# Where chunk 3 is transposed, where raw copies lie, and which bank comes next: three edits in the second layer's projection of a two-layer transformer kernel

## The chip, the cores and the metric

The kernel runs on one core of a Trainium2 chip. The metric is the device time of one execution in microseconds; the median of three runs before the change is 1957.98 us (1957.88 to 1958.28).

The core's engines are named as in the profile: PE (TensorE, matmuls and transposes through the array) with PEld (its weight loads), ACT (ScalarE), DVE (VectorE), POOL (GpSimd) and SP (SyncE, which here only issues DMAs). Each engine works through its own list of instructions in order and waits on semaphores for the others. TensorE writes to eight PSUM banks of 128 x 512 fp32 words; ACT and DVE copy from there to SBUF.

## The reference

Two layers of attention and two of feed-forward alternate, on one sequence of 2048 positions with 448 features, in fp32, with the same weights both times:

```python
x = x + A(layernorm(x))      # 16 heads of 28, one key and one value head for all
x = x + B(layernorm(x))      # (silu(x @ w_gate) * (x @ w_up)) @ w_down, 1792 wide
x = x + A(layernorm(x))
x = x + B(layernorm(x))

def A(x):
    q = x @ wq               # split into 16 heads of 28
    k, v = x @ wk, x @ wv    # 28 wide, shared by the heads
    p = softmax(q @ k.T * 28 ** -0.5)
    return concat(p @ v) @ wo
```

## The kernel before, in words

The sequence is cut into four chunks of 512 positions (`NC`), each of four tiles of 128. To keep fp32 accuracy in matmuls, each operand is split into a high part, rounded to the matmul's format, and the rest (`xh`, `xl`; `wh`, `wl`). A projection of one chunk by 128 columns of weights (`product_T`, L304) is 11 matmuls into one bank: three for each of three blocks of 128 features, and two for the last block of 64, which holds both parts stacked.

A layer's attention has 16 projection steps (`Attention.project`, L496), four chunks by four column blocks `m`; `self.seen` counts them, and this text calls them steps 0 to 15. Step n belongs to chunk n // 4. A column block holds 112 columns of queries and 16 of the keys (m = 2, 3) or of the values (m = 0, 1). A step (`q`, L516) takes a bank, runs the 11 matmuls, and then:

- ACT casts the bank to the high part of the queries (`self.hi`, L538) and copies it whole to a raw tile (L539). The raw tile comes from a pool `stage` of two, which the feed-forward also uses; for chunk 3 of the second layer it is one of four slices of an `xn` tile (L528 to L531).
- SP stores the raw tile's queries to DRAM (`qd`, L540), and its keys to `kt` (L543), or DVE transposes the values (L546) and POOL copies them into `vsb` (L549).
- After steps 6, 10 and 14 TensorE multiplies a chunk's queries with a few keys (`maxima`, L434), and DVE reduces that to a bound for the softmax and SP stores it.

Besides, `self.when` holds what is to be issued after a step of a given number: loads of keys and queries back from DRAM on SP (L398, L421, L432), and their splits on POOL (L135, L136).

The steps need a chunk's normalised rows transposed, features on partitions. In the second layer this is done in two ways. Chunks 0 to 2 go through DRAM: DVE transposes 32 x 32 blocks (`turn_tile`), SP stores them (`send`), loads them back in the wanted order (`load`, L944), and `halved` (L286) splits them, the high parts by casts on ACT (L292, L296), the rests by subtractions on DVE (L293, L302). Chunk 3, which the feed-forward ends with, goes through TensorE: `flip` (L243) makes 16 transposes of 128 x 128, four to a bank, and for each bank ACT casts (L254, L258) and DVE subtracts (L255, L264).

The order is written out by hand; instructions run on each engine in the order in which the Python code issues them. Steps 0 to 3 of the second layer are spread over the last units of the first feed-forward (`hand_over`, L910, through `self.soon`, and `rest`, L1083); the rest follows in `finish` (L553), behind the feed-forward's last products. `hand_over` puts further pieces into `self.plan`, keyed by the step and by 0 (before its matmuls) or 1 (behind them): for chunk 2 the load behind step 4 and the split before step 7, for chunk 3 the last of the normalisation (`ready`: DVE L230, POOL L232) behind step 5. `project` calls `turned` for a chunk before the step ahead of its first and before its first: chunk 3's `flip` comes before step 11. The rows then are TensorE's transposes (L248), ahead of step 11's matmuls.

`bank(cands)` (L111) hands out banks in turn, with one position kept for each list of candidates, and skips those held. `finish` sets the list for steps 4 to 12 and for the flip: 0 to 7 in order. Steps 13 to 15 take 3, 4, 5, and `maxima` has a list of its own. Steps 2 and 3 took banks 1 and 2 of the four low ones, so `used`, of which the change speaks, is 2. Before the change steps 4 to 10 have banks 0 to 6, the flip 7, 0, 1, 2, steps 11 and 12 banks 3 and 4; the three `maxima` have 4, 5, 6.

`halves` (L122) is a pair of 128 x 512 tiles under one tag with two buffers. The feed-forward keeps its product `h` in it (`h2`, L1017), the attention its sums (`o2`, L694).

Behind step 15 the scores begin (`scores`, L566): in each cycle TensorE makes 24 matmuls of scores (L633) and 8 of the products with the values (L688), ACT three exponentials (L655, L656).

Of the kernel before, what the change touches and what calls it, by code (L numbers as in the profile page):

```python
# [8 lines left out]
F32 = mybir.dt.float32  # L9
# [14 lines left out]
NC = S // 512  # L24
# [31 lines left out]
def forward(  # L56
# [32 lines left out]
    LOW, HIGH, ALL = (0, 1, 2, 3), (4, 5, 6, 7), (4, 5, 6, 7, 0, 1, 2, 3)  # L89
    wide = [ALL]  # L90
# [20 lines left out]
    def bank(cands, hold=False):  # L111

        for _ in cands:
            turn[cands] = (turn.get(cands, -1) + 1) % len(cands)
            b = cands[turn[cands]]
            if b not in live:
                if hold:
                    live.add(b)
                return b, banks[b]
        raise AssertionError("no bank")  # L120

    def halves(name):  # L122

        return pers.tile([P, 2, 512], F32R, tag="halves", name=name, bufs=2)
# [151 lines left out]
    def natural(po, squares):  # L276

        if not squares:
            return po
        return po.rearrange("p (g t w) -> p t g w", g=4, w=32)  # L280

    def in_order(a, squares):

        return a.rearrange("p (t g w) -> p t g w", g=4, w=32) if squares else a
# [19 lines left out]
    def product_T(po, a_h, a_l, tiles):  # L304

        xh, xl = tiles[:2]
        seq = []
        for k in range(3):
            seq += [(a_h[k], xh[:, k, :]), (a_h[k], xl[:, k, :]), (a_l[k], xh[:, k, :])]
        seq += [(a_h[3], xh[:, 3, :]), (a_l[3], xh[:, 3, :])]  # L310
        for i, (a, b) in enumerate(seq):
            nc.tensor.matmul(po, a, b, start=(i == 0), stop=(i == len(seq) - 1))
# [30 lines left out]
    class Attention:  # L343
# [152 lines left out]
        def project(self):  # L496

            c, m = self.order[self.seen]
            for f in self.plan.get((self.seen, 0), ()):
                f()  # L500
            late = self.layer == 0 and self.seen == 3
            turned = [self.order[n][0] for n in (self.seen, self.seen + 1) if n % 4 == 0 and n < len(self.order)]
            for o in turned if not late else ():
                self.turned(o)
            self.q(c, m)
            for o in turned if late else ():
                self.turned(o)
            for f in self.plan.get((self.seen, 1), []) + self.when.pop(self.seen, []):
                f()
            self.seen += 1  # L510
# [5 lines left out]
        def q(self, c, m):  # L516
            cs = slice(512 * c, 512 * c + 512)
            sq = c in self.squares
            held, po = bank((3, 4, 5) if self.seen > len(self.order) - 4 else wide[-1], True)
            ms = slice(P * m, P * m + P)  # L520
            wh, wl = self.w
            product_T(po, [wh[:, k, ms] for k in range(4)], [wl[:, k, ms] for k in range(4)], self.X[c])
            if not full and self.seen in (6, 10, 14):
                self.maxima(self.seen // 4 - 1)()
            live.remove(held)
            if c not in self.qd:
                self.qd[c] = dram.tile([D, 512], F32, name=f"qd{self.layer}_{c}")
            if self.layer and c == NC - 1:  # L528
                if "xn" not in self.spare:
                    self.spare["xn"] = pers.tile([P, 4, 512], F32, name="xn")  # L530
                raw = self.spare["xn"][:, self.seen % 4, :]  # L531
            else:
                raw = self.pool.tile([P, 512], F32, name="stage")
            if not full:
                if self.seen % 2 == 0:
                    self.two = wpool.tile([P, 2, 512], F32R, tag="wgh", name="q2", bufs=FG + 1)
                self.hi[c, m] = self.two[0:112, self.seen % 2, :]
                nc.scalar.copy(in_order(self.hi[c, m], sq), natural(po[0:112, :], sq))  # L538
            nc.scalar.copy(in_order(raw, sq), natural(po, sq))  # L539
            nc.sync.dma_start(self.qd[c][112 * m : 112 * m + 112, :], raw[0:112, :])  # L540
            d0, n = 16 * (m % 2), 12 if m % 2 else 16
            if m > 1:
                nc.sync.dma_start(self.kt[c][d0 : d0 + n, :], raw[112 : 112 + n, :])  # L543
                return
            vt = wpool.tile([P, 512], F32R, tag="wgl", name="vt", bufs=FG + 1).bitcast(F32)[96:128, :]
            nc.vector.transpose(vt, po[96:128, :])  # L546
            vt = vt.rearrange("p (u t d) -> p u t d" if sq else "p (t u d) -> p u t d", t=4, u=4)
            for u in range(4):
                nc.gpsimd.tensor_copy(  # L549
                    vsb[32 * u : 32 * u + 32, 4 * c : 4 * c + 4, d0 : d0 + n], vt[:, u, :, 16 : 16 + n]  # L550
                )

        def finish(self):  # L553

            wide.append((0, 1, 2, 3, 4, 5, 6, 7) if self.layer else ALL)
            if self.layer:
                nc.scalar.activation(warm, halfn[:, 0:1], AF.Exp)
            while self.seen < len(self.order):
                self.project()
            for n in sorted(self.when):  # L560
                for f in self.when[n]:
                    f()
            self.advance(len(self.steps), NM + KC * LEAD)
            wide.append(LOW)

        def scores(self, ff, xb):  # L566
            next(switch)
            inner = ExitStack()
            with tc.tile_pool(name=f"ow{self.layer}", bufs=1, side="right", reuse_waits="tile") as ow:
# [56 lines left out]
                def tile_scores(n, three, one):  # L626

                    i, kt = divmod(n, NT)
                    q, k, ks = qts[i % 3], keys[kt // 4], slice(P * (kt % 4), P * (kt % 4) + P)
                    for z, (kp, part) in enumerate(((0, 0), (1, 0), (0, 1))):  # L630
                        for j in (0, 1, 2, 3) if n % 2 else (3, 0, 1, 2):
                            js = slice(32 * j, 32 * j + 32)
                            nc.tensor.matmul(  # L633
                                three[:, j, :] if j < 3 else one, k[js, kp, ks], q[js, part, :],
                                start=(z == 0), stop=(z == 2), tile_position=(32 * j, 0),
                            )
                    pt, pt1 = bufs[n % 4], pairs[n // 2 % 2][:, n % 2, :]
                    pts[n] = [*(pt[:, j, :] for j in range(3)), pt1]
                    return pt, pt1
# [489 lines left out]
    for c in range(1, NC):  # L1129
        fs, got = norm_steps(c)  # L1130
        n = 4 * c - 4
# [38 lines left out]
```

## Time and profile before

| | |
|---|---|
| median of the runs | 1957.98 us |
| the profiled execution | 1958.55 us |
| its span, first to last instruction | 1956.8 us |
| PE busy | 1942.8 us, 99% |
| ACT busy | 1262.7 us, 65% |
| DVE busy | 969.6 us, 50% |
| POOL busy | 553.9 us, 28% |
| granted clock of TensorE, mean | 0.999 |

The profile is one execution, the time of the instructions on each engine. A busy time of TensorE is not all work at full speed: where the granted clock is below 1.00, a matmul takes longer and counts as busy all the same. In the order of time a row has the start, the duration (of the group, where "x3" stands behind it), engine, line, operation, output and inputs by their names in the program, and in brackets the idle time before it with what ended it. A row of stretches has the stretch, its length, the busy time and count of PE, weight loads, DVE, ACT and POOL, the granted clock, the busy share of the DMA engines, and GB/s.

The second layer's projection (steps 4 to 15) lies between 993.59 and 1032.87 us of the span.

### The profile page before, as it was taken

Reading aid. Unit: us, or ns where it says so; the run is one execution under the profiler, and the core shown is the slowest. Engines: PE = TensorE matmul, PEld = TensorE weight load, DVE = VectorE, ACT = ScalarE, POOL = GpSimd, SP = SyncE. Lnnn points to the kernel's source line nnn. Section 1 sums busy time; section 2 is a strip of 40 time slices with the busy share of each in tenths; the row PEclk is TensorE's granted clock in tenths of the full one; section 3 lists DMA queues with packets and bytes.
Section 4 is the critical chain, followed back from the end, with each engine's and each line's share of the span. In section 5 each row is a group of like instructions: output and inputs, shape, how many; then the busy total and the mean of one; then the engine's idle time right before and its main releaser. Section 6 shows DMA issues by size and latency. Waiting matters only on the chain. (4 is left out here: it accounts for less than half of the span.)

```text
span 1956.8 us, 43898 instructions
## 1 busy us (share of the span) xinstructions
PE 1942.8 (99%) x18425; PEld 1328.7 (68%) x18425; DVE 969.6 (50%) x1639; ACT 1262.7 (65%) x1877; POOL 553.9 (28%) x592
## 2 busy tenths in 40 slices
PE   9999999999999999999999999999999999999998
PEld 7544545445468999999974445454454789988887
DVE  6666575665643222322655555657656432232323
ACT  4899898998953333333349998989989333333332
POOL 4213123122214333433341221122231342333420
PEclk9999999999999999999999999999999999999999
DMA  5111011121130011100251110110221201011102
GB/s 167 55 35 30 21 39 41 27 55 39 25 87 25 17 32 32 33 22 22 70 156 36 34 34 20 42 38 24 57 50 32 72 18 31 17 32 32 32 1 77
DMA packets 100642, 83.60 MB, mean 43 GB/s; under 512 B 25080, under 2 KB 81656, under 8 KB 100440
## 3 DMA queue, kind: packets, MB, share of 16 engines
q1 hardware_dynamic: 98744, 79.32, 14.7%
q8 instruction: 145, 2.38, 0.5%
q10 hardware_dynamic: 1696, 1.43, 0.2%
q14 instruction: 57, 0.47, 0.1%
HBM read 57.38 MB, written 21.50 MB: 40 GB/s over the span
## 5 line engine op out<-in xcount | busy, mean ns | idle before, releaser
L655 ACT ACTIVATE pt<-three 128x1536 f32<-128x1536 f32 x512 | 726.9, 1499 | 52.8 <-PE three L633 52.8
L688 PE MATMUL bank<-pt,vsb 128*32 128x512 f32 x3072 | 490.8, 598 | 0.0
L688 PE MATMUL bank<-pair,vsb 128*32 128x512 f32 x1024 | 487.4, 598 | 0.6 <-ACT pair L656 0.6
L633 PE MATMUL bank<-qstack,keys 32*128 32x512 f32 x1536 | 473.3, 425 | 0.0
L332 PE MATMUL bank<-xh,wgh 64*128 64x512 f32 x1712 | 446.7, 389 | 0.0
L633 PE MATMUL three<-qstack,keys 32*128 32x512 f32 x4608 | 428.6, 408 | 0.5 <-ACT xn L539 0.3
L633 PEld LDWEIGHTS bank<-qstack,keys 32*128 32x128 f32 x1536 | 243.3, 183 | 250.4 <-issue 123.3
L654 DVE COPY pair<-bank 128x512 f32<-128x512 f32 x512 | 354.2, 692 | 95.2 <-PE bank L633 58.9
L332 PE MATMUL bank<-xh,wgl 64*128 64x512 f32 x1391 | 368.3, 390 | 0.0
L332 PE MATMUL bank<-xl,wgh 64*128 64x512 f32 x1284 | 335.2, 389 | 0.0
L332 PE MATMUL bank<-wdh,h 64*128 64x448 f32 x1760 | 328.3, 363 | 0.0
L1022 DVE TENSOR_TENSOR sg<-bank,sg 128x512 f32<-128x512 f32 x112 | 77.4, 691 | 500.7 <-ACT sg L1021 495.8
L656 ACT ACTIVATE pair<-pair 128x1024 f32<-128x1024 f32 x256 | 285.4, 1115 | 0.0
L332 PEld LDWEIGHTS bank<-xh,wgh 64*128 64x128 f32 x1712 | 265.1, 184 | 15.6 <-issue 1.3
L633 PEld LDWEIGHTS three<-qstack,keys 32*128 32x128 f32 x4608 | 261.0, 183 | 13.9 <-DVE xres L604 1.5
L688 PEld LDWEIGHTS bank<-pt,vsb 128*32 128x32 f32 x3072 | 101.7, 109 | 246.2 <-issue 153.2
L896 POOL TENSOR_TENSOR xres<-stage,xres 128x448 f32<-128x448 f32 x107 | 126.5, 1204 | 492.8 <-ACT stage L895 492.6
L697 DVE TENSOR_TENSOR o<-bank,o 128x512 f32<-128x512 f32 x224 | 154.9, 692 | 203.7 <-PE bank L688 203.7
L332 PEld LDWEIGHTS bank<-wdh,h 64*128 64x128 f32 x1760 | 244.6, 184 | 11.6 <-issue 2.0
L339 ACT COPY seen<-bank 128x1 f32<-128x1 f32 x654 | 80.7, 163 | 250.4 <-PE bank L332 247.5
L332 PEld LDWEIGHTS bank<-xh,wgl 64*128 64x128 f32 x1391 | 218.1, 184 | 13.4
L332 PE MATMUL bank<-wdl,h 64*128 64x448 f32 x880 | 218.3, 366 | 0.0
(149 smaller groups left out, 2118.8 us busy)
## 6 DMA issues: line engine op xcount, KB each, us to landing
o<-rd SPq DMA_DIRECT2D x32, 256.0 KB
qraw<-qd SPq DMA_DIRECT2D x128, 56.0 KB
qd<-stage SPq DMA_DIRECT2D x28, 224.0 KB
wdr<-in_B_w_down_dram SPq DMA_DIRECT2D x28, 224.0 KB
xt<-tb SPq DMA_DIRECT2D x24, 224.0 KB
wr<-in_B_w_gate_dram SPq DMA_DIRECT2D x28, 192.0 KB
wr<-in_B_w_up_dram SPq DMA_DIRECT2D x28, 192.0 KB
xn<-xt SPq DMA_DIRECT2D x6, 768.0 KB
```

The lines of the kernel that those rows point to most:

```text
L332: nc.tensor.matmul(po, a, b, start=start, stop=stop, skip_group_check=True)
L339: nc.scalar.copy(seen[:, i : i + 1], po[:, 0:1])
L633: nc.tensor.matmul(three[:, j, :] if j < 3 else one, k[js, kp, ks], q[js, part, :], start=(z == 0), stop=(z == 2), tile_position=(32 * j, 0),)
L654: copies.append(nc.vector.tensor_copy(pt1, one))
L655: es.append(nc.scalar.activation(pt, threes[y], AF.Exp, scale=SCALE))
L656: es.append(nc.scalar.activation(pair, pair, AF.Exp, scale=SCALE))
L688: nc.tensor.matmul(to[32 * j : 32 * j + 32, :], vsb[:, n % NT, :], pts[n][j], start=(y == 0), stop=(y == 1), skip_group_check=True,)
L697: f = nc.vector.tensor_tensor(accs[i][:, 0, :], to, accs[i][:, 0, :], ALU.add)
L896: nc.gpsimd.tensor_tensor(r, s, r, ALU.add)
L1022: nc.vector.tensor_tensor(in_order(sg, sq), natural(pg[1], sq), in_order(sg, sq), ALU.mult)
```

## The change

Three edits, all of which act in the second layer alone (`self.layer` is 1):

- before step 8, `project` transposes chunk 3 (`NC - 1`), and no longer before step 11, where `turned` finds the chunk's rows gone and does nothing;
- the raw tiles of steps 4 to 11 are the two halves of a `halves` pair, a new pair at each even step, instead of `stage` tiles (chunk 3, steps 12 to 15, keeps its `xn` slices);
- `q` notes the bank that it held, and `finish` makes the list of banks from it: the four low ones, beginning with the one behind the last used, and then 4 to 7. With `used` = 2 that is 3, 0, 1, 2, 4, 5, 6, 7.

With it steps 4 to 7 have banks 3, 0, 1, 2, the flip 4 to 7, steps 8 to 11 again 3, 0, 1, 2, step 12 bank 4.

```diff
@@ project
             late = self.layer == 0 and self.seen == 3
             turned = [self.order[n][0] for n in (self.seen, self.seen + 1) if n % 4 == 0 and n < len(self.order)]
+            if self.layer and self.seen == 8:
+                turned = [NC - 1]
             for o in turned if not late else ():
                 self.turned(o)
             self.q(c, m)
@@ q
             product_T(po, [wh[:, k, ms] for k in range(4)], [wl[:, k, ms] for k in range(4)], self.X[c])
+            self.used = held
             if not full and self.seen in (6, 10, 14):
                 self.maxima(self.seen // 4 - 1)()
@@ q
                     self.spare["xn"] = pers.tile([P, 4, 512], F32, name="xn")
                 raw = self.spare["xn"][:, self.seen % 4, :]
+            elif self.layer and self.seen > 3:
+                if self.seen % 2 == 0:
+                    self.spare["raw"] = halves("raw").bitcast(F32)
+                raw = self.spare["raw"][:, self.seen % 2, :]
             else:
                 raw = self.pool.tile([P, 512], F32, name="stage")
@@ finish
-            wide.append((0, 1, 2, 3, 4, 5, 6, 7) if self.layer else ALL)
+            wide.append((*((self.used + n) % 4 for n in range(1, 5)), *HIGH) if self.layer else ALL)
```

## The prediction

> **What bounds the kernel now.** I read the page first (busy time, slices), then busy time by stretch around the second layer's projection, then the order of time of each engine there. A "step n" is the projection counted n in the code (16 steps per layer).
>
> The page's engine rows say that TensorE is what the time is made of, and ScalarE what it alternates with:
>
> ```profile
> PE 1942.8 (99%) x18425; PEld 1328.7 (68%) x18425; DVE 969.6 (50%) x1639; ACT 1262.7 (65%) x1877; POOL 553.9 (28%) x592
> ```
>
> Only 14.0 us of the span of 1956.8 are without a matmul, so a change that removes waits has little to win. The stretches (length, then busy time of PE, weight loads, DVE, ACT, POOL, then granted clock) show where the change's stage stands in this:
>
> ```profile
> 8.00:12.00 4.00, 2.65 (x19) 1.84 (x18) 1.78 (x4) 2.88 (x5) 2.82 (x6) 1.00 0.51 118
> 1004.85:1007.24 2.39, 0.50 (x1) 0.19 (x1) 2.26 (x6) 1.67 (x3) 0.64 (x1) 0.98 0.93 261
> 1007.24:1010.70 3.46, 3.46 (x8) 2.76 (x9) 1.93 (x3) 1.19 (x3) 1.93 (x4) 0.52 0.54 176
> 1034.00:1100.00 66.00, 65.89 (x724) 30.23 (x728) 40.06 (x65) 66.00 (x56) 8.15 (x9) 1.00 0.11 30
> 1580.00:1950.00 370.00, 370.00 (x3306) 329.66 (x3303) 109.36 (x160) 118.65 (x445) 112.12 (x91) 1.00 0.10 29
> ```
>
> From 1004.85 to 1007.24 TensorE has 0.50 us of work, and in the 3.46 us behind it "busy" hides a loss: the clock is 0.52. From 1034 on ScalarE is busy without a gap (66.00 of 66.00), and the last stage is matmul without a gap (370.00 of 370.00). So what the projection wins or loses moves the start of the scores, and the end of the kernel with it. TensorE's rows, in order of time (start, duration, what; in brackets the idle time before and its releaser):
>
> ```profile
> 1004.46 0.39 PE L312 MATMUL bank<-xh,wl 128*128 128x512 f32 x1
> 1006.13 0.50 PE L312 MATMUL bank<-xh,wh 128*128 128x512 f32 x1 [1.29 <-ACT xh L292]
> 1007.24 0.80 PE L312 MATMUL bank<-xl,wh 128*128 128x512 f32 x1 [0.60 <-DVE xl L293]
> ...
> 1010.94 0.39 PE L312 MATMUL bank<-xh,wl 128*128 128x512 f32 x1
> 1011.17 0.40 PE L312 MATMUL bank<-xh,wh 128*128 128x512 f32 x1
> ...
> 1016.18 1.10 PE L438 MATMUL bank<-q,kdiag 112*128 112x512 f32 x4
> 1017.11 1.91 PE L248 MATMUL bank<-ident,xn 128*128 128x128 f32 x16
> 1018.78 0.48 PE L312 MATMUL bank<-xh,wh 128*128 128x512 f32 x1
> ...
> 1023.67 0.39 PE L312 MATMUL bank<-xh,wl 128*128 128x512 f32 x1
> 1024.17 0.50 PE L312 MATMUL bank<-xh,wh 128*128 128x512 f32 x1
> 1024.51 0.40 PE L312 MATMUL bank<-xl,wh 128*128 128x512 f32 x1
> ...
> 1032.87 0.49 PE L633 MATMUL bank<-qstack,keys 32*128 32x512 f32 x1
> ```
>
> Step 7 ends with the matmul at 1004.46; step 8, the first of chunk 2, starts at 1006.13 and step 9 at 1011.17, where 11 matmuls at the undisturbed spacing (1010.94 to 1011.17, 0.23) would have taken 2.5 us. The transposes of chunk 3 take 1017.11 to 1018.78, ahead of step 11. Step 13 starts 0.27 us late (1023.67 + 0.23 = 1023.90, it starts at 1024.17). A first matmul behind a break has 0.1 us more to its second (1024.17 to 1024.51: 0.34). The scores begin at 1032.87.
>
> **The change part by part.** *The transposes move from before step 11 to before step 8.* They leave their old place: 1.67 us, and the 0.1 us of the restart behind them: 1.77 us. In the new place they run from 1004.46 + 0.23 = 1004.69 to 1006.36. They need chunk 3's normalised rows and a free bank; the rows of ScalarE, VectorE and GpSimd in that stretch:
>
> ```profile
> 1005.47 1.86 ACT L292 CAST xh<-qstack 128x512 fp32r<-128x512 f32 x3 [1.85 <-DMA qstack<-xt]
> 1007.74 0.62 ACT L296 CAST xh<-qstack 128x512 fp32r<-128x512 f32 x1 [0.41 <-DMA qstack<-xt]
> 1008.27 0.58 ACT L538 CAST q<-bank 112x512 fp32r<-112x512 f32 x1
> 1011.71 0.59 ACT L539 COPY stage<-bank 128x512 f32<-128x512 f32 x1 [2.86 <-DMA kt<-stage]
> 1012.19 0.59 ACT L538 CAST q<-bank 112x512 fp32r<-112x512 f32 x1
> ...
> 1017.86 1.57 ACT L254 CAST xh<-bank 128x512 fp32r<-128x512 f32 x3
> 1019.30 0.63 ACT L258 CAST xh<-bank 128x512 fp32r<-128x512 f32 x1
> ```
>
> ```profile
> 1003.39 0.70 DVE L440 STREAM_TRANSPOSE sg<-bank 128x512 f32<-128x512 f32 x1
> ...
> 1006.50 1.98 DVE L293 TENSOR_TENSOR xl<-qstack,xh 128x512 fp32r<-128x512 f32 x3
> 1008.51 0.69 DVE L302 TENSOR_TENSOR xh<-qstack,xh 64x512 fp32r<-64x512 f32 x1
> 1012.33 0.72 DVE L546 STREAM_TRANSPOSE vt<-bank 32x512 f32<-32x512 f32 x1 [3.13 <-ACT stage L539]
> ...
> 1020.51 1.89 DVE L255 TENSOR_TENSOR xl<-bank,xh 128x512 fp32r<-128x512 f32 x3
> 1022.43 0.69 DVE L264 TENSOR_TENSOR xh<-bank,xh 64x512 fp32r<-64x512 f32 x1
> 1023.39 0.72 DVE L546 STREAM_TRANSPOSE vt<-bank 32x512 f32<-32x512 f32 x1 [0.26 <-issue]
> ```
>
> ```profile
> 1002.27 1.51 POOL L232 COPY xn<-xn 128x64 f32<-128x64 f32 x4 [0.61 <-DVE xn L230]
> ```
>
> The rows are whole at 2.27 + 1.51 = 1003.78. The first bank the transposes take is that of the maxima before, read by L440 until 1004.09. Both are ahead of 1004.69, by 0.9 and 0.6 us; were that cover gone, each tenth past it would come off the start of step 8 only beyond the next bound.
>
> That bound is the load of chunk 2, which the change doesn't hasten. Step 8's first matmul can go at 1006.36 (its operand is cast by 1005.47 + 1.86/3 = 1006.09). Its second needs the first of the three subtractions, 1006.50 + 0.66 = 1007.16: it goes at 1007.24, as now. The third comes 0.34 later, the next six 0.23 apart, to 1008.96; the tenth needs L302 (1008.51 + 0.69 = 1009.20), so 1009.26; the eleventh 0.33 later, and step 9 at 1009.82. Against 1011.17 that is 1.35 us, if the clock stays full.
>
> *The clock.* It went to 0.52 behind two idle times, 1.29 and 0.60 us, with one matmul between. In the new order only 1006.75 to 1007.24 (0.5 us) is idle there. The row of 8 to 12 us has 1.35 us idle and a clock of 1.00, so 0.5 should leave it. The ends are 1.35 us (full clock) and 0 (half clock until the same moment, 1010.70: step 9 then stays at 1011.17). I take 1.35: 0.5 is far from 1.9 and below 1.35. [...]
>
> *What the transposes carry with them on the other queues.* On ACT four casts (1017.86 to 1019.93, 2.07 us) go ahead of step 8's two copies, on DVE four subtractions (1020.51 to 1023.12, 2.61 us) behind step 7's transpose L546. No DMA and no GpSimd work moves. ACT: step 7's cast ends at 1008.85, its raw copy follows at once (below), to 1009.4, the four casts to 1011.5, step 8's cast to 1012.1, its raw copy to 1012.7, where that cast now starts at 1012.19: ACT is level with before by step 9, with TensorE 1.35 us ahead. DVE: L546 at 1009.4 instead of 1012.33, the subtractions by 1012.8; its next work is the maxima of step 10, about 1015.6. Chunk 3 is ready some 5 us before step 12 (1018.3). Cost: nothing, hidden in ACT's 2.86 us and DVE's 3.13 us of waiting.
>
> *Raw copies into the double buffers of h, steps 4 to 11.* Two pairs give four places instead of two. Steps 4 to 7 no longer wait for stores; step 7's copy loses its 2.86 us. Steps 8 and 9 take the first pair and wait for the stores of steps 4 and 5, the last of which landed at 1011.71 and leaves SP in the same order: hence the raw copy above no earlier than 1011.71. The pairs' former contents (h of the last two units) are read by matmuls that stand ahead of step 4 in TensorE's own order. TensorE waits for none of these copies in the trace except through a bank.
>
> *Banks by last use.* Step 13 takes bank 3, now that of step 11 (the list of L555 turned on by L113 to L119), whose L546 ends at 1023.39 + 0.72 = 1024.11, hence 1024.17. After the change bank 3 belongs to steps 4 and 8, empty by 1012.7. The wait goes: 0.27 + 0.11 of restart = 0.38 us. Step 14's bank (4, step 12) is as near as before; next late is the scores' own start behind step 15's copies, unchanged.
>
> Sum: 1.77 + 1.35 + 0.38 = 3.50 us. The profiled execution took 1958.55 us, 1.75 outside its span, 0.57 above the median of the runs; it would become 1955.05, and the median 1957.98 - 3.50 = 1954.5.
>
> **The rivals.** *1, the clock halves all the same:* step 8 goes on at half speed until 1010.70, whatever stood before it, step 9 stays at 1011.17, and the gain is 1.77 + 0.38 = 2.15: 1955.8. For it: the one matmul of half a microsecond before 1007.24 may not count as activity, and the trace can't show what a transpose counts; against it: 1.35 us idle at full clock.
>
> *2, chunk 2's load lands earlier:* step 8 follows the transposes unbroken, ends 0.87 us sooner (1006.36 + 0.1 + 2.5 = 1008.95 for step 9), 1953.6. Against it: the load's place in SP's queue is the same, and two ACT rows wait for it (1.85, 0.41).
>
> *3, it does not do what it says:* the transposes are held (bank or rows) until chunk 2 is in, and run before step 8 outside the gap. Then 1.67 is lost there and 1.77 + 0.38 won elsewhere: 1957.5. For it only margins of 0.6 and 0.9 us.
>
> *4, slower:* step 8's raw copy waits for both stores of a whole pair, and everything on ACT is behind it. TensorE feels it when step 13 wants bank 3, at 1009.82 + 4 x 2.5 + 0.93 for the maxima (1016.18 to 1017.11) = 1020.75. To lose what is won this copy would have to be released 3.5 us past that, at about 1024.2 instead of 1011.71; at 1028.2 the kernel would be 0.2% slower, 1962. Against it: the last of the four stores had landed at 1011.71, by ACT's own row, and nothing is put ahead of it on SP.
>
> **How the numbers follow.** Forecast 0.70 (own range 1954.0 to 1955.1, for the clock's edge and the restarts), rival 1 0.13, rival 2 0.06, rival 3 0.06, rival 4 0.05. The range 1953.5 to 1956.8 takes in the forecast and rivals 1 and 2. 0.2% is 3.9 us, about what a measurement of this kernel can tell from no change: faster is rival 2 and the forecast's edge, 0.12; slower most of rival 4, 0.05; the rest, 0.83, lies within.
>
> **What would show it.** Right: 16 transposes at about 1004.7 and 1.7 us long; step 8's second matmul still at 1007.2, behind L293; a clock of 1.00 from 1007 to 1011; step 9 at 1009.8; step 11 straight behind the maxima at 1015.7; step 13 without a wait; the scores at 1029.4 instead of 1032.87, and the same length from there to the end. Wrong: a clock of 0.5 there (rival 1), transposes waiting for a bank or GpSimd (3), a raw copy on ACT past 1020 (4), or a later stage that eats the 3.5 us.

## The result, and the profile after

The changed kernel takes 1954.86 us (median of 19 runs, 1954.06 to 1957.93) beside 1958.49 us for the kernel before on the same chip (19 runs, 1957.73 to 1963.68). The ratio is 0.998, with a 95% interval of 0.9974 to 0.9987: 3.6 us faster by the medians, and inside 0.2%. The prediction had 1954.5 and 3.50 us.

The profiled execution took 1956.43 us, 1.6 above that median. Its rows around the second projection stand 1.64 us later than those before (step 7's last matmul at 1006.10, where it was 1004.46), for a reason at the start of the kernel that the last section shows. So rows of the two kernels are compared here by their distance from step 7's last matmul. TensorE, in order of time (start, duration, instruction; in brackets the idle time before it and its releaser):

```profile
1006.10 0.39 PE L312 MATMUL bank<-xh,wl 128*128 128x512 f32 x1
1006.33 1.91 PE L248 MATMUL bank<-ident,xn 128*128 128x128 f32 x16
1007.99 0.48 PE L312 MATMUL bank<-xh,wh 128*128 128x512 f32 x1
1008.90 0.50 PE L312 MATMUL bank<-xl,wh 128*128 128x512 f32 x1 [0.42 <-DVE xl L293]
...
1011.47 0.40 PE L312 MATMUL bank<-xh,wh 128*128 128x512 f32 x1
...
1016.50 1.10 PE L438 MATMUL bank<-q,kdiag 112*128 112x512 f32 x4
1017.43 0.40 PE L312 MATMUL bank<-xh,wh 128*128 128x512 f32 x1
...
1022.44 0.39 PE L312 MATMUL bank<-xh,wh 128*128 128x512 f32 x1
...
1030.97 0.50 PE L640 MATMUL bank<-qstack,keys 32*128 32x512 f32 x1
```

The transposes follow step 7 without a break. Of the two waits at step 8 one of 0.42 us is left. Step 9 (1011.47) is 5.37 us behind the mark, where it was 6.71. Step 11 follows the maxima at once, step 13 (1022.44) has no wait, and the scores begin 24.87 us behind the mark, where it was 28.41: 3.54 us won. From there to the end of the span it is 1954.7 - 1030.97 = 923.7 us, before 1956.8 - 1032.87 = 923.9: nothing is given back.

The busy time by stretch after the change (length, then busy PE, weight loads, DVE, ACT, POOL, then granted clock):

```profile
1006.50:1008.90 2.40, 1.98 (x18) 1.66 (x16) 2.27 (x6) 1.75 (x3) 0.65 (x1) 1.00 0.87 236
1008.90:1012.36 3.46, 3.46 (x14) 2.63 (x15) 3.37 (x6) 3.16 (x8) 1.93 (x4) 1.00 0.57 181
1012.36:1030.97 18.61, 18.61 (x82) 15.04 (x81) 9.85 (x17) 7.90 (x15) 14.06 (x30) 1.00 0.52 157
1032.00:1098.00 66.00, 65.80 (x720) 30.11 (x720) 40.10 (x64) 66.00 (x56) 8.82 (x9) 1.00 0.11 30
```

In 3.46 us, where TensorE did 8 matmuls at a clock of 0.52, it now does 14 at 1.00; and behind it there is no idle time at all up to the scores. ScalarE after the change:

```profile
1007.08 1.82 ACT L292 CAST xh<-qstack 128x512 fp32r<-128x512 f32 x3 [2.45 <-DMA qstack<-xt]
...
1010.21 0.59 ACT L546 COPY raw<-bank 128x512 f32<-128x512 f32 x1
1010.68 1.57 ACT L254 CAST xh<-bank 128x512 fp32r<-128x512 f32 x3
1012.11 0.63 ACT L258 CAST xh<-bank 128x512 fp32r<-128x512 f32 x1
1012.59 0.64 ACT L545 CAST q<-bank 112x512 fp32r<-112x512 f32 x1
1013.38 0.59 ACT L546 COPY raw<-bank 128x512 f32<-128x512 f32 x1
```

Step 7's raw copy (1010.21) no longer waits for a store, the four casts of chunk 3 follow it, and step 8's raw copy starts at 1013.38 - 1.64 = 1011.74 on the time scale of before, where step 5's keys landed at 1011.71 (its row names no releaser, so that it waits for them is not shown).

### The profile page after: what moved, and what is told of

Its sections match the earlier page's. It is cut to its first block, busy times and chain, and to the rows that moved or that the text cites. A ratio compares the mean times of both kernels' runs of the same rounds, so it can differ in the third digit from the quotient of the medians.

```text
span 1954.7 us, 43894 instructions
## 1 busy us (share of the span) xinstructions
PE 1942.0 (99%) x18425; PEld 1325.5 (68%) x18425; DVE 970.0 (50%) x1639; ACT 1261.9 (65%) x1877; POOL 552.8 (28%) x592
## 5 line engine op out<-in xcount | busy, mean ns | idle before, releaser
L663 ACT ACTIVATE pair<-pair 128x1024 f32<-128x1024 f32 x256 | 280.6, 1096 | 0.0
```

The source lines that it names most:

```text
L663: es.append(nc.scalar.activation(pair, pair, AF.Exp, scale=SCALE))
```

## The experiments

Each was read in two ways: its time against the kernel before on the same chip, and its TensorE rows. The table has the starts in us behind step 7's last matmul; the last column is the length to the first matmul of the scores, the mark in the expectations.

| kernel | step 8 | step 9 | 12 | 13 | 14 | 15 | scores |
|---|---|---|---|---|---|---|---|
| before | 1.67 | 6.71 | 16.95 | 19.71 | 22.38 | 25.81 | 28.41 |
| after | 1.89 | 5.37 | 13.85 | 16.34 | 18.83 | 22.27 | 24.87 |
| flip_only | 1.89 | 5.37 | 13.81 | 20.70 | 24.87 | 28.32 | 30.93 |
| flip_raw | 1.89 | 5.37 | 13.82 | 16.31 | 18.81 | 22.24 | 24.85 |
| flip_banks | 1.89 | 5.36 | 13.82 | 16.31 | 21.63 | 26.76 | 29.38 |
| raw_banks | 2.45 | 6.97 | 17.19 | 19.68 | 22.18 | 25.61 | 28.21 |
| raw_only | 1.85 | 6.19 | 17.05 | 19.58 | 22.23 | 25.66 | 28.26 |
| banks_only | 1.58 | 6.77 | 17.03 | 19.52 | 22.02 | 25.45 | 28.05 |
| filler | 1.89 | 5.37 | 15.62 | 18.83 | 21.36 | 24.80 | 27.40 |
| half | 1.75 | 5.38 | 14.73 | 17.70 | 20.22 | 23.65 | 26.26 |
| quarter | 1.69 | 5.33 | 15.11 | 18.15 | 20.67 | 24.11 | 26.71 |
| load_early | 1.89 | 5.36 | 13.82 | 16.31 | 18.81 | 22.24 | 24.85 |
| rows_late | 2.33 | 5.54 | 14.01 | 16.50 | 19.00 | 22.43 | 25.03 |
| both | 1.89 | 4.50 | 12.94 | 15.44 | 17.93 | 21.37 | 23.97 |

### The transposes alone

The first of the three edits, without the others: raw copies in `stage` tiles, banks 0 to 7.

```diff
 turned = [self.order[n][0] for n in (self.seen, self.seen + 1) if n % 4 == 0 and n < len(self.order)]
+if self.layer and self.seen == 8:
+    turned = [NC - 1]
```

> Chunk 3's transposes before step 8, raw copies in the stage tiles and banks in order as before. The mark is the length from step 7's last matmul to the first matmul of the scores: 28.41 us before (1004.46 to 1032.87), 24.87 with all three edits (1006.10 to 1030.97). Theory 'the terms add' (the prediction's): 28.41 - 1.77 - 1.35 = 25.3, and a time 3.1 us below before. Rival 'the stores bind': step 11's raw copy still waits for the store of step 9's keys, which leaves SP behind the load of keys and lands 18 us behind the mark (1022.7 in the profile before), so step 13 gets bank 3 no sooner than before: 28.0 to 28.4, and the time of before.

Measured: 1960.9 us beside 1958.94 (ratio 1.0008, 0.9999 to 1.0018), and 30.93 us from the mark to the scores, 2.5 more than before. Neither theory had it this long. Up to step 12 everything is won that was predicted (13.81 against 16.95). Then, in TensorE's rows:

```profile
1020.56 0.39 PE L312 MATMUL bank<-xh,wl 128*128 128x512 f32 x1
1025.18 0.79 PE L312 MATMUL bank<-xh,wh 128*128 128x512 f32 x1 [4.23 <-DVE vt L549]
1025.77 0.63 PE L312 MATMUL bank<-xl,wh 128*128 128x512 f32 x1
```

Step 13 wants bank 3 and stands 4.23 us for the transpose of step 11's values. What that waits for is on ScalarE (first fence), and the store in question on SP (second):

```profile
1011.95 0.59 ACT L542 COPY stage<-bank 128x512 f32<-128x512 f32 x1 [2.98 <-DMA kt<-stage]
...
1017.88 0.59 ACT L542 COPY stage<-bank 128x512 f32<-128x512 f32 x1 [0.96 <-DMA kt<-stage]
1018.49 0.59 ACT L541 CAST q<-bank 112x512 fp32r<-112x512 f32 x1
1023.73 0.58 ACT L542 COPY stage<-bank 128x512 f32<-128x512 f32 x1 [4.65 <-DMA kt<-stage]
```

```profile
1017.79 0.43 SPq L546 DMA_DIRECT2D kt<-stage  x1
```

Step 11's raw copy stands 4.65 us until step 9's keys, issued at 1017.79, have landed: 5.9 us for 32 KB. TensorE had become faster, and the landing did not come sooner for it: it came 19.25 us behind the mark, where it was 18.26 (1022.72 - 1004.46). So step 11 waits for what step 9 left behind. The rival had this wait, and left out two things: the landing 1 us later, for which no run shows the reason, and a second bill. Behind the idle time the granted clock is 0.61 over 4.22 us, where it was 0.99:

```profile
1020.60:1025.18 4.58, 0.35 (x2) 0.00 (x0) 0.72 (x1) 1.45 (x3) 0.63 (x3) 0.99 0.51 154
1025.18:1029.40 4.22, 4.22 (x12) 3.36 (x13) 0.72 (x1) 0.11 (x1) 3.65 (x10) 0.61 0.36 109
```

From step 13 to 14 it then takes 4.17 us instead of 2.50. The wait of 4.39 us (20.70 against 13.81 + 2.50) and this 1.67 are the 6.06 us by which the length stands above that of all three edits.

### The transposes with the pairs, and with the banks

> The transposes before step 8 and the raw copies in the pairs, banks in order as before. 'The terms add': the 0.38 us of the banks is missing, 25.3. 'The stores bind': with no raw copy waiting for a store, step 11's bank 3 is empty before step 13 asks for it, and the banks are worth nothing beside the pairs: 24.9, 3.5 us below before.

Measured: 1955.44 us beside 1958.94 (0.9983, 0.9974 to 0.9993), length 24.85, the changed kernel's to 0.02. With the pairs, the banks are worth nothing here.

> The transposes before step 8 and the banks by last use, raw copies in the stage tiles. 'The terms add': the pairs had no term of their own, 24.9. 'The stores bind': step 13 finds bank 3 empty, but ACT stands at step 11's raw copy until the same store has landed, step 12's bank 4 is emptied behind it, and step 14 waits for that: 26.5 to 26.8, 1.6 to 1.9 us below before.

Measured: 1959.49 us (1.0, 0.9991 to 1.001), length 29.38. Step 13 finds its bank, as both theories have it, but step 14 does not: ScalarE stands at step 11's raw copy as above, and step 12's bank, which it would empty behind that, comes late.

```profile
1025.77 0.52 PE L312 MATMUL bank<-xh,wh 128*128 128x512 f32 x1 [2.66 <-DVE vt L549]
```

The 2.8 us of this wait (21.63 against 18.81) and 1.7 us of a lower clock behind it (0.67 from 1025.77 to 1031.00; 14 to 15 takes 5.13, where it is 3.43 with the maxima between) make 4.5, the distance to the changed kernel. The stores bind; moving the bank moves the wait by one step.

### The pairs and the banks without the transposes

> The pairs and the banks, the transposes left before step 11. Both theories: only step 13's wait goes, 28.03; step 8 with the same gap (1.29 and 0.60 us) and the clock at half behind it. If the clock stays full here, the gap was not its cause, and the length is 26.7.

> The pairs alone: transposes before step 11, banks in order as before. Step 13 still takes step 11's bank 3. If the store that step 11's raw copy waits for made bank 3 late, that wait goes with the pairs as it does with the banks: 2.5 us from step 12's first matmul to step 13's, where it was 2.76 before. If it needs the banks: 2.76 as before. The gap at step 8 and the half clock stay in any case, step 9 at 6.7 to 7.0 behind step 7's last matmul.

> The banks by last use alone: transposes before step 11, raw copies in the stage tiles. Step 13 gets a bank that has long been empty: 2.5 us from step 12's to step 13's first matmul, and a length of 28.0. ACT still stands at step 11's raw copy (0.5 us before); if that now holds up step 14, whose bank 4 is emptied behind it, 13 to 14 is longer than 2.5.

Measured: raw_banks 1958.07 us beside 1958.94 (0.9992, 0.9982 to 1.0001), length 28.21; raw_only and banks_only, one execution each, lengths 28.26 and 28.05. Step 12 to 13 is 2.49, 2.53 and 2.49 where it was 2.76: either edit takes that wait away, and together they do it once. In raw_only step 14 then starts 0.15 late, and the length gains 0.15 against 0.36. raw_banks is 0.16 longer than banks_only; chunk 2's load landed later in its execution (step 8 at 2.45 instead of 1.58). All three keep the gap at step 8 and a lower clock behind it (0.57 in raw_banks, 0.68 in raw_only, 0.56 in banks_only, over some 3.5 us).

### What the transposes are worth as activity

The pairs and banks, chunk 3's transposes left before step 11, and 16 transposes of the identity in the new place; they are added work, and nothing reads them.

```diff
+if self.layer and self.seen == 8:
+    for n in range(16):
+        nc.tensor.transpose(banks[7][:, 0:P], ident, ident)
```

> The pairs and the banks, chunk 3's transposes left before step 11, and in their new place 16 transposes of the identity into a bank that nobody reads: work for TensorE in the gap that brings nothing. If the activity in the gap keeps the clock up (the prediction's term of 1.35 us): a clock of 1.00 from step 8 on, step 9 some 5.36 us behind step 7's last matmul, and a length of 28.03 - 1.35 = 26.7. If the clock does not depend on that gap: half clock behind it, step 9 at 6.71 as before, 28.03.

Measured: step 9 at 5.37 as in the changed kernel, at a clock of 1.00 from 1006.77 to 1010.20: the term of 1.35 us comes of the filled gap, also where the work in it is useless. The length is 27.40, 0.7 more than expected: with steps 9 and 10 earlier and the real transposes where they were, chunk 3's subtractions on VectorE, behind the maxima of step 10, come too late for step 12 (a wait of 0.34 us for L255, and more behind it). The time (1958.67 beside 1959.03; 0.9999, 0.9989 to 1.0008) can't tell this from before. So 1.35 us of earlier steps is not 1.35 us of the kernel while the transposes stay ahead of step 11.

Half of the transposes (two banks of four), then a quarter, ahead of step 8, the others before step 11:

```diff
+if self.layer and self.seen == 8:
+    flip(self.norms[NC - 1], self.X[NC - 1], (0, 1))     # half; (0,) in quarter
 def turned(self, c):
     if c in self.norms:
-        flip(self.norms.pop(c), self.X[c])
+        flip(self.norms.pop(c), self.X[c], (2, 3) if self.layer else range(4))     # (1, 2, 3) in quarter
```

> All three edits, but only half of the transposes (two of four banks) before step 8, the other half before step 11. The gap then has 0.8 and some 0.5 us idle. If that little leaves the clock up, as the 1.35 us idle in the first layer did: 24.87 + 0.84 + 0.1 = 25.8. If it halves behind it: step 9 at 6.71, 27.2.

> All three edits, one of the four banks of transposes before step 8, three before step 11. About 1.5 us of 2.4 are then idle around step 8's first matmul, between the 1.0 that left the clock up and the 1.9 that halved it. Clock full: step 9 at 5.4 behind step 7's last matmul. Clock halved: 6.7 to 7.0. [...]

Measured: half 1956.75 us beside 1959.03 (0.9988, 0.9978 to 0.9997), length 26.26; quarter, one execution, 26.71. In both step 9 is at 5.4 and the clock behind the gap 1.00 (half 1010.63 to 1014.10, quarter 1007.34 to 1010.80). half is 0.5 us longer than expected, for filler's reason: from step 12 to 13 it takes 2.97 us instead of 2.50 (VectorE's last two subtractions end at 1024.18 and 1024.90, and the matmuls behind them start at 1024.24 and 1024.96). The stretches from step 7's end to step 8's second matmul, and the 3.5 us behind them, for quarter, raw_only, banks_only and raw_banks:

```profile
1004.97:1007.34 2.37, 0.93 (x6) 0.38 (x4) 2.24 (x6) 1.71 (x3) 0.65 (x1) 1.00 1.01 277
1007.34:1010.80 3.46, 3.46 (x14) 2.63 (x15) 3.33 (x5) 2.67 (x5) 1.93 (x4) 1.00 0.54 176
```

```profile
1005.00:1007.39 2.39, 0.51 (x1) 0.19 (x1) 2.26 (x6) 1.54 (x3) 0.65 (x1) 1.00 0.94 273
1007.39:1010.90 3.51, 3.51 (x11) 2.79 (x12) 2.64 (x4) 1.80 (x4) 1.93 (x4) 0.68 0.53 171
```

```profile
1005.25:1007.65 2.40, 0.49 (x2) 0.19 (x2) 2.26 (x6) 1.75 (x3) 0.65 (x1) 1.00 0.85 248
1007.65:1011.20 3.55, 3.55 (x9) 2.86 (x10) 1.92 (x3) 1.10 (x2) 1.93 (x4) 0.56 0.57 184
```

```profile
1004.79:1007.58 2.79, 0.51 (x3) 0.19 (x2) 2.27 (x6) 1.40 (x3) 0.99 (x2) 0.93 0.94 240
1007.58:1011.10 3.52, 3.52 (x9) 2.84 (x10) 2.64 (x4) 1.84 (x4) 1.24 (x3) 0.57 0.52 167
```

With 1.44 us idle of 2.37 the clock stays at 1.00; with 1.88 of 2.39, 1.91 of 2.40 and 2.28 of 2.79, as with 1.89 of 2.39 before the change, it falls (to 0.68, 0.56, 0.57 and 0.52 in the stretches behind). That alone does not put an edge between 1.44 and 1.88 us. In the traces before and after the change the moments at which the granted clock changes lie a whole number of spans of 3.413 us apart: before, it goes down at 1007.16, up at 1010.57, and down at 1956.06, 277 spans later; after, down at 11.42, up at 18.24, two spans later, and down at 1953.60, 567 spans later. Counted by such spans, which is an estimate where no change is near, quarter's idle time is divided between two. Its only change after the start of the kernel is at 1954.95, and counted back from there the boundaries fall at 1002.63, 1006.05 and 1009.46. The two spans of quarter, and the one ahead of the fall in raw_only:

```profile
1002.63:1006.05 3.42, 2.77 (x15) 2.09 (x13) 3.25 (x9) 0.93 (x2) 1.24 (x4) 1.00 0.93 286
1006.05:1009.46 3.41, 2.62 (x10) 1.70 (x11) 3.32 (x6) 3.13 (x7) 2.57 (x4) 1.00 0.80 219
```

```profile
1005.22:1008.63 3.41, 1.74 (x6) 1.21 (x7) 3.28 (x6) 2.76 (x5) 1.80 (x3) 1.00 0.88 251
```

quarter has 0.65 and 0.79 us idle in them and keeps its clock. The span ahead of the fall has 1.67 us idle in raw_only, 1.82 before the change, 1.91 in banks_only and 2.06 in raw_banks. half has 1.03 us in one span (1008.59 to 1012.00) and keeps its clock. In filler the span from 1004.04 to 1007.45 has 0.43 us idle with the 16 transposes of 1.7 us in it, and would have some 2.1 without them (0.43 + 1.7, an estimate); its clock stayed at 1.00, so these transposes counted as activity, which the prediction left open. Around step 8, then, spans with up to 1.03 us idle kept the clock, and those with 1.67 us or more lost it. Where the boundaries fall in the gap differs from one execution to the next (before the change the clock goes down at 1007.16, 0.08 us before the gap ends, in raw_only at 1008.63, 1.24 us behind its end, hence the 0.68 above); that this decides as well is the author's estimate from quarter. There is one profiled execution of each kernel. All four with the whole gap lost the clock; whether every execution of the kernel before does is not shown.

### What bounds step 8 now

```diff
-                a.plan[4, 1] = [load]
+                a.plan[4, 0] = [load]
```

> All three edits, and chunk 2's load is issued before step 4's products, not behind its stores. If the load bounds step 8: its casts begin up to 1 us sooner, and the length falls by as much, to 23.9. If DVE's queue bounds it (the maxima's reductions and step 6's transpose are ahead of the subtractions): step 8's second matmul stays at 2.8 us behind step 7's last, 24.8.

Measured: 1955.51 us beside 1959.03 (0.9985, 0.9975 to 0.9994), length 24.85: nothing. The load came sooner (its first cast at 1007.06, 0.47 us behind the mark instead of 0.98), and VectorE didn't. In its rows the subtractions follow the maxima's reductions and step 6's transpose without a gap, 2.04 us behind the mark (1006.59), as in the changed kernel (1008.15 - 1006.10 = 2.05):

```profile
1007.53 0.31 DVE L451 STREAM_TRANSPOSE flat<-two 128x128 f32<-128x128 f32 x1
1007.88 0.72 DVE L553 STREAM_TRANSPOSE vt<-bank 32x512 f32<-32x512 f32 x1
1008.63 1.98 DVE L293 TENSOR_TENSOR xl<-qstack,xh 128x512 fp32r<-128x512 f32 x3
```

The other bound alone, and both (what moves is four reductions of VectorE, 1.6 us from 1004.13 on before the change; the expectation counts five and 2.3):

```diff
-self.maxima(self.seen // 4 - 1)()
+rows = self.maxima(self.seen // 4 - 1)
+if self.layer and self.seen == 6:
+    self.plan[7, 1] = [rows]
+else:
+    rows()
```

> All three edits, and the maxima's reductions of step 6 behind step 7, but the load where it was. If DVE's queue alone bounds step 8's second matmul, that wait goes, and the length is 24.0 as with both. If the load's last part bounds the tenth matmul behind it (its cast waited 0.3 us for the DMA), only some 0.3 us go: 24.5.

> As the kernel with the load issued before step 4's products, and the maxima's reductions of step 6 (five small DVE instructions, 2.3 us with what lies between) are issued behind step 7, so that the subtractions of chunk 2 go ahead of them. Both bounds of step 8 are then gone: it follows the transposes without a break, 24.87 - 0.87 = 24.0. If there is a third bound, it shows as the releaser of step 8's matmuls, and the length stays near 24.8.

Measured: rows_late, one execution, has a length of 25.03: VectorE was free 1.92 us before the first cast, but in this execution chunk 2's load landed 1.66 us behind the mark instead of 0.98 (first cast at 1006.11, mark 1004.45), and step 8 waited for it. That the load bounds it in this execution is shown; the 0.3 us expected are not, since the landing differs by more from one execution to the next. Both together: 1954.41 us beside 1959.03 (0.9974, 0.9964 to 0.9983), length 23.97, 0.90 below the changed kernel. TensorE's rows have no wait left at step 8:

```profile
1004.87 1.91 PE L248 MATMUL bank<-ident,xn 128*128 128x128 f32 x16
1006.53 0.47 PE L312 MATMUL bank<-xh,wh 128*128 128x512 f32 x1
1006.84 0.39 PE L312 MATMUL bank<-xl,wh 128*128 128x512 f32 x1
```

It is the fastest kernel of this study; beside load_early, which ran on the same chip and has the changed kernel's length, it is 1.1 us faster by the medians.

## Why the prediction was right, and what in it was not

*The sum.* 3.50 us, measured 3.54 in the profile and 3.6 by the medians. By its steps, in us behind the mark: step 9 was put at 5.36 (it is at 5.37), step 11 at 11.29 (11.33), step 13 at 16.29 (16.34), the scores at 24.91 (24.87).

*The transposes' new place.* Right: no wait for bank or rows; step 8's second matmul where it was, behind L293, at 2.80 (2.78 before); the tenth matmul late by 0.05 us. What the prediction named as the bound there, the load, was not the one that held: with the load 0.5 us sooner (load_early) nothing moves, since VectorE's queue holds the subtractions back. Only when VectorE is free does the load bind (rows_late), and with both out of the way step 8 follows at once. Rival 2, the load landing earlier, was priced at 0.87 and would not have come from the load alone.

*The clock.* Right, 1.35 us, and filler shows that it is the filled gap that does it (step 9 at 5.37 us, before 6.71). Before the change 1.89 us idle in 2.39, with a matmul in between, were followed by a clock of 0.50 for 3.41 us (1007.16 to 1010.57); with the gap filled it is 1.00 from 1008.90 to 1012.36, and rival 1, by which it halves all the same, falls.

*The work carried along on ACT and DVE.* Right: ScalarE's raw copy of step 8 at 1011.74 on the old clock (predicted not before 1011.71), VectorE's subtractions done at 1013.55 + 0.70 - 1.64 = 1012.6 (1012.8). VectorE's row:

```profile
1013.55 0.70 DVE L264 TENSOR_TENSOR xh<-bank,xh 64x512 fp32r<-64x512 f32 x1
```

*The step that failed: "Raw copies into the double buffers of h", which had no term, and "Banks by last use", which had 0.38.* The sum came out right, its parts did not. The 0.38 is there alone (0.36 in banks_only) but is not the banks' in company: flip_raw, without them, is as fast. The wait behind it was the store's already before the change, since the pairs alone remove it too (step 12 to 13 takes 2.53 us in raw_only, 2.76 before). And the pairs, at nothing, carry the whole gain: without pairs and banks the moved transposes make the kernel 2.5 us longer in the profile instead of 3.1 shorter, and from flip_only to flip_raw is 6.08 us. That the sum holds is luck in so far as the pairs were part of the change: by its terms flip_banks would have won the same 3.50 us, and its length is 0.97 us above that of before. "TensorE waits for none of these copies in the trace except through a bank" was true of the trace before, where step 11's copy waited 0.52 us for its store. What was not asked is what that wait becomes when TensorE comes 3 us earlier and the store does not. Rival 4 had the place (bank 3 at step 13, behind ScalarE's raw copy) but put it on the pairs, which remove it, and left out the half clock that follows it.

## What to carry to other kernels

A wait that is short in the trace because everything comes late together grows when one makes the rest earlier (step 11's copy here from 0.52 us to 4.65): before an edit is costed at nothing, shift the rows by the expected gain and look at each store, load and buffer that doesn't shift with them. Parts of a change are not terms of a sum when one makes room for another; here the transposes and the pairs are worth 3.5 us of the profile together, -2.5 (transposes) and 0.15 (pairs) apart. The gap in TensorE's work at step 8 cost itself and, where 1.67 us or more of it lay in one span of 3.41 us (1.03 us did not do it), a lower clock in the next: before the change 0.50 for 3.41 us, by which step 9 came 1.34 us later than with the gap filled. Useful work pulled into the gap saved both.

## What the runs showed beside this

The profiled execution of the changed kernel lost its 1.64 us in the first 20 us of the span, where the change has no part. TensorE's stretches there, after the change:

```profile
6.50:10.50 4.00, 1.68 (x11) 0.88 (x8) 2.43 (x6) 1.48 (x3) 2.53 (x6) 1.00 0.67 114
10.50:17.50 7.00, 6.61 (x23) 5.18 (x24) 5.31 (x11) 4.02 (x9) 4.95 (x10) 0.57 1.00 380
```

It idles 2.3 us of the first 4, and the clock is 0.57 for 7 us; the first exponential of the first layer's scores then starts at 66.78 instead of 64.99. Before the change TensorE idles 1.25 us in the same first 4, and the clock stays at 1.00. The work is the same in both kernels, its speed in these two executions is not: the first 36 transposes take 5.61 us after the change and 6.81 before, so that TensorE then waits 2.04 us instead of 1.07 for VectorE's rows. The span ahead of the fall (8.00 to 11.42) has 1.47 us idle. At the start of other kernels spans with 1.49 and 1.53 us idle (rows_late, quarter; mean clock of the execution 0.999 and 1.000) kept the clock and one with 1.38 (load_early; 0.998) lost it, so the profile's idle time does not fix the edge more closely than this. One and the same stretch lost the clock in one of these two executions and kept it in the other, and at step 7's last matmul the two profiles stand 1.64 us apart, almost half of what this change is worth. A single profiled execution's total would have misjudged it; the distances between rows of one stage did not.
